# FFN gate and up computed as rows of 384 columns and turned back, and all q rows in one PSUM tile, in a decode-attention kernel

## Chip, cores, metric

One NeuronCore of a Trainium2 chip. The metric is device time in microseconds (us) of the one core. The kernel before takes 297.3 us (median of 3 runs, 297.22 to 297.4).

## The reference, cut

```python
# B = 2 sequences, one token each, D = 640, 32 heads of 192, window of 2048 keys, F = 1536
h  = x + attention(layernorm(x), k_cache, v_cache, wq, wo)   # scores and softmax over the last 2048 keys
h2 = h + (gelu(layernorm(h) @ w_gate) * (layernorm(h) @ w_up)) @ w_down
```

K and V of the window are 2 x 32 x 2048 x 192 bf16 values each, about 50 MB each. With the weights the core has to read 122.3 MB. The arithmetic for two tokens is small.

## The kernel before

All loads go through one ring of 120 KB per partition, from one DMA queue, in a fixed order: the first K tile, wq, then K and V tiles in turn with wo's four parts between, then w_gate, w_up and w_down. A load is issued as soon as the ring's place is free. For each K tile PE makes transposes, scores and the product with V; these hide behind the loads. At the very end comes the FFN: hnT, the second layernorm's output turned into columns, goes into gate and up; uT, the product of GELU(gate) and up, goes into w_down; h_rows adds h to the output's bank. Each matmul below is two records of PE, a weight load and a product. Two more words of the DMA packets: a packet of the kind "instruction" is a fetch of an engine's instructions, and a completion write is the 4-byte packet with which one of the 16 DMA engines ends its part of a load. Queue q1 carries the loads; q8 brings PE's instructions, one packet of 16384 bytes for about 265 PE records on average; q14 brings other instructions.

q, before: four PSUM tiles, four copies, 48 products that turn q into stationaries.

```python
for J in range(4):                      # q rows: 80 products in all
    for r in range(4):
        e.matmul(tps[J][32*r:32*(r+1), 0:384], lhsT=xnT[:, c, :], rhs=wq[...], tile_position=(0, 32*r))
# ... four ACT copies qrow[:, J] <- tps[J]; then for each J, hl, k (48 products):
e.matmul(ops_[:, col:col+15:2], lhsT=qx[:, o:o+255:2], rhs=selq[:, :])
```

FFN, before: the weights are the stationary, the result comes out in columns, so nothing has to be turned.

```python
def ffn_in(bank, key):                  # 60 products of 2 columns, for gate and again for up
    for f in range(NF):
        for c in range(NC5):
            e.matmul(bank[:, 2*f:2*f+2], lhsT=wv[:, c, 512*(f//4)+f%4 : 512*(f//4)+512 : 4], rhs=hnT[:, c, :])
# gate -> gsb -> GELU on DVE and ACT -> ga ; h_rows ; up -> uT = up * ga
for i, (f0, f1) in enumerate(WDC):      # ((0,4),(4,8),(8,10),(10,12)): 4 loads of w_down
    e.matmul(m1[32*r:32*r+2, 0:160], lhsT=uT[:, f, :], rhs=wd[...], tile_position=(0, 32*r))
# yrow <- m1, two stores of the output
```

A helper records the operations and adds the semaphore waits. Two engines that use the same PSUM bank are always put in order (the X list of an operation names the banks).

Of the kernel before, what the change touches and what calls it, by code (L numbers as in the profile page):

```python
# [12 lines left out]
B = 2  # L13
# [133 lines left out]
WDC = ((0, 4), (4, 8), (8, 10), (10, 12))  # L147
# [3 lines left out]
def bass_sequential_preLN__sliding_block_cached__geglu_ffn__decode_kernel(  # L151
# [12 lines left out]
    with ExitStack() as ctx:  # L164
# [23 lines left out]
        selq = sb("selq", [128, 8], BF16)  # L188
# [3 lines left out]
        bits = sb("bits", [128, 10], I32)  # L192
        pti = sb("pti", [128, 10], I32)
        pf = sb("pf", [128, 10], F32)
# [13 lines left out]
        xnT = sb("xnT", [128, NC5, 32], BF16)  # L208
        hnT = sb("hnT", [128, NC5, B], BF16)
        hT = sb("hT", [128, NC5, B], F32)  # L210
        qrow = sb("qrow", [128, 4, 2, 2, DH], BF16)
# [17 lines left out]
        hsel = sb("hsel", [128, 2, B], F32)  # L229
        gsb = sb("gsb", [128, NF * B], F32)  # L230
# [63 lines left out]
        def load_ffn():  # L294
            for key, w in (("wg", B_w_gate), ("wu", B_w_up)):
                load(key, 2 * NC5 * F, w.rearrange("(p c) f -> p c f", c=NC5),
                     lambda v: v.rearrange("p (c f) -> p c f", c=NC5))
            wd = B_w_down.rearrange("(i p s) n -> i p s n", p=128, s=4)
            for i, (f0, f1) in enumerate(WDC):
                load(("wd", i), 2 * (f1 - f0) * D, wd[f0 // 4, :, f0 % 4:f0 % 4 + f1 - f0, :],  # L300
                     lambda v: v.rearrange("p (s n) -> p s n", n=D))
# [38 lines left out]
        BITS = (1, 2, 3, 12, 16, 28, 31, 32, 64, 96)  # L340
# [18 lines left out]
        def layernorm(src, src_tok, dst, dst_tok):  # L359
# [14 lines left out]
            dve(tt(dst[:, :, 0:B], dT[:, 0, :, :], lt[:, 1, :].unsqueeze(1).to_broadcast([128, NC5, B]), ALU.mult),  # L374
                R=["dT0", "lt1"], W=[dst_tok])

        def _x_T(e):
# [7 lines left out]
        layernorm(xT, "xT", xnT, "xnT")  # L385


        dve(tt(pti[:, :], pi[:, :].to_broadcast([128, 10]), bits[:, :], ALU.bitwise_and),
            R=["pi"] + [("bits", k) for k in range(10)], W=["pti"])
# [20 lines left out]
        dve(ts(pg[:, 9:10], rb(31), 4.0, ALU.mult, pg[:, 8:9], ALU.add), R=["pf", "cq"], W=["cqb"])  # L410
# [4 lines left out]
        dve(ts(selq[:, :], cf[:, 0, 0:8], pg[:, 9:10], ALU.is_equal), R=["cf0", "cqb"], W=["selq"])  # L415
# [62 lines left out]
        def q_rows():  # L478
            for i, (c0, c1) in enumerate(WQC):
                wq, wtoks = where["wq", i]  # L480

                def fn(e, c0=c0, c1=c1, wq=wq):
                    for c in range(c0, c1):
                        for J in range(4):
                            for r in range(4):
                                ins = e.matmul(tps[J][32 * r:32 * (r + 1), 0:384], lhsT=xnT[:, c, :],  # L486
                                               rhs=wq[:, c - c0, 1536 * J + 384 * r:1536 * J + 384 * (r + 1)],
                                               start=(c == 0), stop=(c == NC5 - 1), tile_position=(0, 32 * r))
                    return ins

                pe(fn, R=["xnT"] + wtoks, X=[("t", J) for J in range(4)])
                done(("wq", i))
            for J in range(4):
                act(lambda e, J=J: e.activation(  # L494
                    out=qrow[:, J, :, :, :],
                    in_=tps[J][:, 0:384].rearrange("p (h d) -> p h d", h=2).unsqueeze(2).to_broadcast([128, 2, 2, DH]),
                    func=ACT.Copy, scale=SCALE), W=[("qrow", J)], X=[("t", J)])

        def q_stationary():
            for J in range(4):  # L500
                def fn(e, J=J):
                    for hl in range(2):
                        qx = qrow[:, J, hl, :, :].rearrange("p r d -> p (r d)")
                        for k in range(6):
                            col = 96 * J + 16 * k + hl
                            o = 256 * (k // 2) % DH + k % 2
                            ins = e.matmul(ops_[:, col:col + 15:2], lhsT=qx[:, o:o + 255:2], rhs=selq[:, :],  # L507
                                           start=True, stop=True)
                    return ins

                pe(fn, R=[("qrow", J), "selq"], X=["o"])
            for g in range(NG):
                x = 4 * (2 * (g % 2) + g % 4 // 2)
# [260 lines left out]
```

## Time and profile before

| what | value | view |
|---|---|---|
| time | 297.3 us | runs |
| span of the profiled execution | 295.3 us | page |
| main DMA queue | 97.1% of 16 engines' span, 122.29 MB | page, part 3 |
| chain of waits | DMA 74%, PE 19% | page, part 4 |
| hnT ready to uT started | 283.24 to 288.31, 5.07 us | timeline |
| last down products released | 292.17 us | timeline, chain |

From the page of the kernel before: the busy line; the clock granted to PE and the data rate in 40 slices of the span; the DMA queues (packets, MB, share of 16 engines); the shares of the chain of waits by engine; and one line of DMA issues (count, size, median time from issue to landing).

```profile
PE 199.6 (68%) x2251; PEld 158.1 (54%) x2251; DVE 126.9 (43%) x313; ACT 99.8 (34%) x126; POOL 2.7 (1%) x18
...
PEclk9998758997979589977888599979597979597565
...
GB/s 267 443 457 422 429 426 422 426 428 429 425 438 431 439 429 422 426 422 424 425 435 436 429 433 428 432 426 426 432 429 425 429 428 429 429 425 425 422 391 65
...
q1 hardware_dynamic: 6488, 122.29, 97.1%
q8 instruction: 17, 0.28, 0.4%
q14 instruction: 3, 0.02, 0.0%
...
DMA 74%; PE 19%; DVE 3%; ACT 2%; SPq 1%; issue 0%
...
ring<-in_A_k_cache_dram SPq DMA_DIRECT2D x16, 3072.0 KB, 27.2
```

The rate does not fall between the first slice and the last two. A K tile lands 27 us after its issue although 3 MB take about 7.3 us at this rate, so several transfers always stand in the queue; a computation that ends a few us earlier in the middle lets nothing arrive earlier. What remains is the end. From the timeline of the kernel before (start, duration, engine, line, operation, output and inputs, count, and in brackets what ended the idle time before it):

```profile
283.07 0.17 DVE L323 TENSOR_TENSOR hnT<-dT,lt 128x10 bf16<-128x10 f32 x1 [1.01 <-ACT lt L373]
283.30 2.16 PE L675 MATMUL sps<-hnT,ring 128*128 128x2 bf16 x60 [0.79 <-DVE hnT L323]
...
286.04 2.16 PE L675 MATMUL ops<-hnT,ring 128*128 128x2 bf16 x60
...
288.31 0.18 DVE L323 TENSOR_TENSOR uT<-ops,ga 128x24 bf16<-128x24 f32 x1 [0.96 <-PE ops L675]
...
288.55 0.70 PE L705 MATMUL m<-ring,uT 128*2 128x160 bf16 x16 [0.34 <-DVE uT L323]
...
290.59 1.23 PE L705 MATMUL m<-ring,uT 128*2 128x160 bf16 x24 [1.33 <-DMA ring<-in_B_w_down_dram]
...
292.17 0.44 PE L705 MATMUL m<-ring,uT 128*2 128x160 bf16 x8 [0.35 <-DMA ring<-in_B_w_down_dram]
292.66 0.32 DVE L711 CAST yrow<-m 98x160 bf16<-98x160 f32 x1 [4.17 <-PE m L705]
293.01 0.65 SPq L713 DMA_DIRECT2D out_dram<-yrow  x1
```

uT is there at 288.5, but PE then waits for w_down three times. The chain of waits (start, length, what) says the same:

```profile
263.40 28.73 DMA ring<-in_B_w_down_dram
292.13 0.04 issue
292.17 0.47 PE m L705 x8
```

The 48 down products without the waits would end near 290.3 instead of 292.6: the FFN has some 2.3 us of slack behind the last load. And why does that load land so late? The single DMA packets in the trace answer it. 15 of the 16 engines have finished by 290.2 us. One goes on alone, 2560 bytes every 0.10 us, to 291.69. Its two packets of 5120 bytes before that took 547 and 349 ns instead of 199, and they follow directly on an instruction fetch of 16384 bytes that ran from 288.16 to 289.23:

```
kernel before, packets (start us, ns, bytes):
288.16 1071 16384 (queue 8, instruction)   289.21 547 5120   289.75 349 5120
then 2560 bytes at 290.10 290.20 290.30 ... 291.59, one at a time; last completion write 291.69
```

### The profile page before, as it was taken

Reading aid. Unit: us, or ns where it says so; the run is one execution under the profiler, and the core shown is the slowest. Engines: PE = TensorE matmul, PEld = TensorE weight load, DVE = VectorE, ACT = ScalarE, POOL = GpSimd, SP = SyncE. Lnnn points to the kernel's source line nnn. Section 1 sums busy time; section 2 is a strip of 40 time slices with the busy share of each in tenths; the row PEclk is TensorE's granted clock in tenths of the full one; section 3 lists DMA queues with packets and bytes.
Section 4 is the critical chain, followed back from the end, with each engine's and each line's share of the span. In section 5 each row is a group of like instructions: output and inputs, shape, how many; then the busy total and the mean of one; then the engine's idle time right before and its main releaser. Section 6 shows DMA issues by size and latency. Waiting matters only on the chain.

```text
span 295.3 us, 5104 instructions
## 1 busy us (share of the span) xinstructions
PE 199.6 (68%) x2251; PEld 158.1 (54%) x2251; DVE 126.9 (43%) x313; ACT 99.8 (34%) x126; POOL 2.7 (1%) x18
## 2 busy tenths in 40 slices
PE   2583659849495397849591697567696876785773
PEld 1461348729293385538471676364676674753461
DVE  5940274725255154434344156335266434252230
ACT  2150316625253062516261244334244344241000
POOL 3000000000000000000000000000000000000000
PEclk9998758997979589977888599979597979597565
DMA  7999999999999999999999999999999999999991
GB/s 267 443 457 422 429 426 422 426 428 429 425 438 431 439 429 422 426 422 424 425 435 436 429 433 428 432 426 426 432 429 425 429 428 429 429 425 425 422 391 65
DMA packets 6520, 122.60 MB, mean 415 GB/s; under 512 B 738, under 2 KB 740, under 8 KB 1252
## 3 DMA queue, kind: packets, MB, share of 16 engines
q1 hardware_dynamic: 6488, 122.29, 97.1%
q8 instruction: 17, 0.28, 0.4%
q14 instruction: 3, 0.02, 0.0%
q10 hardware_dynamic: 12, 0.00, 0.0%
HBM read 122.29 MB, written 0.00 MB: 414 GB/s over the span
## 4 chain that ended last, share of the span: by engine, by line
DMA 74%; PE 19%; DVE 3%; ACT 2%; SPq 1%; issue 0%
DMA ring<-in_A_k_cache_dram 54%; PE tps L464 17%; DMA ring<-in_B_w_down_dram 10%; DMA ring<-in_A_wq_dram 9%; SPq L268 1%; ACT qrow L494 1%; PE ops L565 1%; DVE rq L323 1%; ACT ktr L473 1%; PE m L611 0%; PE m L594 0%; PE m L549 0%; PE tps L486 0%; DVE ktr L476 0%; DVE cf L323 0%
## 5 line engine op out<-in xcount | busy, mean ns | idle before, releaser
L464 PE MATMUL tps<-identf,ring 128*128 128x128 f32 x768 | 118.6, 325 | 48.1 <-DMA ring<-in_A_k_cache_dram 47.6
L464 PEld LDWEIGHTS tps<-identf,ring 128*128 128x128 f32 x768 | 109.4, 171 | 51.4 <-DMA ring<-in_A_k_cache_dram 48.9
L473 ACT ACTIVATE ktr<-tps 128x1024 bf16<-128x1024 bf16 x80 | 79.5, 1023 | 86.9 <-PE tps L464 86.9
L476 DVE COPY ktr<-tps 128x1024 bf16<-128x1024 bf16 x112 | 74.2, 688 | 76.4 <-PE tps L464 75.4
L540 ACT ACTIVATE eexp<-sm,nm 128x512 bf16<-128x512 f32 x16 | 11.5, 722 | 63.4 <-DVE nm L538 63.4
L529 DVE CUSTOM_DVE_ANT_1 sm<-sps,mska 128x512 f32<-128x512 f32 x16 | 11.1, 691 | 38.7 <-PE sps L523 38.7
L565 PE MATMUL ops<-ring,ering 128*32 128x384 bf16 x512 | 23.9, 328 | 3.6 <-DMA ring<-in_A_v_cache_dram 3.5
L523 PE MATMUL sps<-ktr,rq 128*16 128x512 bf16 x384 | 25.9, 404 | 0.4 <-DVE rq L323 0.4
L565 PEld LDWEIGHTS ops<-ring,ering 128*32 128x32 bf16 x512 | 12.5, 96 | 11.8 <-DMA ring<-in_A_v_cache_dram 4.6
L523 PEld LDWEIGHTS sps<-ktr,rq 128*16 128x16 bf16 x384 | 9.4, 90 | 11.3 <-issue 2.0
L536 PEld LDWEIGHTS m<-mrhs,pm 128*128 128x128 bf16 x16 | 1.5, 96 | 24.4 <-DVE mrhs L319 23.3
L536 PE MATMUL m<-mrhs,pm 128*128 128x16 bf16 x16 | 2.9, 184 | 16.9 <-DVE mrhs L319 16.1
L486 PE MATMUL tps<-ring,xnT 128*32 128x384 bf16 x80 | 5.1, 406 | 7.0 <-DMA ring<-in_A_wq_dram 5.8
L323 DVE TENSOR_TENSOR rq<-ops,mask 128x96 bf16<-128x96 f32 x16 | 2.7, 245 | 15.2 <-PE ops L507 15.2
L323 DVE TENSOR_TENSOR ering<-m,mask 128x256 bf16<-128x256 f32 x16 | 6.7, 420 | 3.2 <-PE m L549 3.2
L486 PEld LDWEIGHTS tps<-ring,xnT 128*32 128x32 bf16 x80 | 2.3, 113 | 9.6 <-DMA ring<-in_A_wq_dram 6.9
L323 DVE TENSOR_TENSOR orow<-m,wm 128x1536 bf16<-128x1536 f32 x4 | 7.0, 1757 | 0.1
L494 ACT ACTIVATE qrow<-tps 128x768 bf16<-128x768 f32 x4 | 2.9, 816 | 11.0 <-PE tps L486 11.0
L594 PE MATMUL m<-selb,orow 128*128 128x2 bf16 x48 | 3.5, 200 | 4.1 <-DVE orow L323 2.5
L371 ACT ACTIVATE lt<-m,eps_t 128x2 f32<-128x2 f32 x2 | 0.5, 262 | 16.5 <-PE m L369 16.5
L549 PE MATMUL m<-sel,eexp 128*128 128x64 bf16 x64 | 5.0, 206 | 1.2 <-ACT eexp L540 1.2
L594 PEld LDWEIGHTS m<-selb,orow 128*128 128x128 bf16 x48 | 3.2, 163 | 4.6 <-DVE orow L323 2.6
(100 smaller groups left out, 85.8 us busy)
## 6 DMA issues: line engine op xcount, KB each, us to landing
ring<-in_A_k_cache_dram SPq DMA_DIRECT2D x16, 3072.0 KB, 27.2
ring<-in_A_v_cache_dram SPq DMA_DIRECT2D x16, 3072.0 KB, 29.6
ring<-in_A_wo_dram SPq DMA_DIRECT2D x4, 1920.0 KB, 30.9
ring<-in_A_wq_dram SPq DMA_DIRECT2D x2, 3072.0 KB, 21.1
ring<-in_B_w_gate_dram SPq DMA_DIRECT2D x1, 1920.0 KB, 33.8
ring<-in_B_w_up_dram SPq DMA_DIRECT2D x1, 1920.0 KB, 24.6
ring<-in_A_wq_dram SPq DMA_DIRECT2D x1, 1536.0 KB, 27.9
ring<-in_B_w_down_dram SPq DMA_DIRECT2D x2, 640.0 KB, 26.9
```

The source lines that it names most:

```text
L323: return lambda e: e.tensor_tensor(out=out, in0=a, in1=b, op=op)
L464: ins = e.transpose(tps[bi][:, 128 * u:128 * (u + 1)], kv[:, off:off + 128], identf[:, :])
L473: act(lambda e, dst=dst, bv=bv: e.activation(out=dst, in_=bv, func=ACT.Copy), W=[("kt", slot, n)], X=[("t", bi)])
L476: dve(lambda e, dst=dst, bv=bv: e.tensor_copy(dst, bv), W=[("kt", slot, n)], X=[("t", bi)])
L486: ins = e.matmul(tps[J][32 * r:32 * (r + 1), 0:384], lhsT=xnT[:, c, :], rhs=wq[:, c - c0, 1536 * J + 384 * r:1536 * J + 384 * (r + 1)], st ...
L494: act(lambda e, J=J: e.activation(out=qrow[:, J, :, :, :], in_=tps[J][:, 0:384].rearrange("p (h d) -> p h d", h=2).unsqueeze(2).to_broadca ...
L523: ins = e.matmul(sps[32 * ch:32 * ch + 16, :], lhsT=rq[:, g, k, :], rhs=ktr[:, g % 2, k // 2, 1024 * ch + k % 2:1024 * (ch + 1):2], start= ...
L529: dve(lambda e: e.tensor_tensor_reduce(out=sm[:, :].rearrange("p (u x) -> p u x", u=4), in0=sps[:, :].rearrange("p (u x) -> p u x", u=4), ...
L540: act(lambda e: e.activation(out=eexp[:, :], in_=sm[:, :], func=ACT.Exp, bias=nm[:, 0:1], scale=1.0, accum_out=zr[:, g // 4 % 2, g % 4:g % ...
L549: ins = e.matmul(o, lhsT=eexp[:, 128 * u:128 * (u + 1)], rhs=sel64[:, :], start=True, stop=True)
L565: ins = e.matmul(ops_[32 * r:32 * (r + 1), 0:384], lhsT=ering[:, g % 4, t, :], rhs=vv[:, 384 * t:384 * (t + 1)], start=(g % 4 == 0 and t < 4),
L594: ins = e.matmul(m2[:, 2 * kk:2 * kk + 2], lhsT=orow[:, :, kk:DH:12], rhs=selb[:, :], start=True, stop=True)
```

## The change

Its intent is fewer and longer PE instructions. q: all rows of all heads in one PSUM tile, one copy instead of four, 12 products instead of 48. FFN: gate and up in 20 products of 384 columns each, in four column groups, instead of 60 products of two columns; the price is that the result stands in rows and has to be copied out of PSUM and turned back by three transposes. w_down is loaded in four equal parts. PE has 110 weight loads and 110 products fewer. Cut to its core:

```diff
-WDC = ((0, 4), (4, 8), (8, 10), (10, 12))
+WDC = ((0, 3), (3, 6), (6, 9), (9, 12))
-        BITS = (1, 2, 3, 12, 16, 28, 31, 32, 64, 96)
+        BITS = (1, 2, 3, 6, 12, 16, 28, 31, 32, 64, 96)
-        dve(ts(pg[:, 9:10], rb(31), 4.0, ALU.mult, pg[:, 8:9], ALU.add), R=["pf", "cq"], W=["cqb"])
+        dve(ts(pg[:, 9:10], rb(6), rb(1), ALU.add), R=["pf"], W=["cqa"])
+        dve(ts(pg[:, 9:10], pg[:, 9:10], 4.0, ALU.mult, pg[:, 8:9], ALU.add), R=["cqa", "cq"], W=["cqb"])
 # q rows: xnT now holds the two tokens four times at different columns, so that J picks the row
-    ins = e.matmul(tps[J][32 * r:32 * (r + 1), 0:384], lhsT=xnT[:, c, :], ...
+    ins = e.matmul(tps[0][32 * r:32 * (r + 1), 0:384], lhsT=xnT[:, c, 32 * J:32 * (J + 1)], ...
 # ... one ACT copy for all J, 12 products for the stationaries instead of 48 ...
+        def ffn_in(bank, xt, key):
+            wv, wtoks = where[key]
+            def fn(e):
+                for c in range(NC5):
+                    for r in range(4):
+                        ins = e.matmul(bank[32 * r:32 * r + 2, 0:384], lhsT=hnT[:, c, :], rhs=wv[:, c, 384 * r:384 * (r + 1)],
+                                       start=(c == 0), stop=(c == NC5 - 1), tile_position=(0, 32 * r))
+                return ins
+            pe(fn, R=["hnT"] + wtoks, X=[xt])
+        def ffn_columns(bank, xt, i):
+            act(lambda e: e.activation(out=grow[0:98, 192:384], in_=bank[0:98, 192:384], func=ACT.Copy), W=[("grow", 1)], X=[xt])
+            dve(lambda e: e.tensor_copy(grow[0:98, 0:192], bank[0:98, 0:192]), W=[("grow", 0)], X=[xt])
+            def fn(e):
+                for j in range(3):
+                    ins = e.transpose(tps[i][:, 128 * j:128 * j + 98], grow[0:98, j:384:3], identf[0:98, 0:98])
+                return ins
+            pe(fn, R=[("grow", 0), ("grow", 1), "identf"], X=[("t", i)])
 # order: gate, h_rows, gate's columns, GELU ; up, up's columns, uT ; down
```

More of the change, by code (lines that the diff above doesn't have):

```diff
@@ L187, in bass_sequential_preLN__sliding_block_cached__geglu_ffn__decode_kernel @@
         sel64 = sb("sel64", [128, 64], BF16)
-        selq = sb("selq", [128, 8], BF16)
+        selq = sb("selq", [128, 32], BF16)
         selb = sb("selb", [128, 2], BF16)
@@ L191, in bass_sequential_preLN__sliding_block_cached__geglu_ffn__decode_kernel @@
         pi = sb("pi", [128, 1], I32)
-        bits = sb("bits", [128, 10], I32)
-        pti = sb("pti", [128, 10], I32)
-        pf = sb("pf", [128, 10], F32)
+        bits = sb("bits", [128, 11], I32)
+        pti = sb("pti", [128, 11], I32)
+        pf = sb("pf", [128, 11], F32)
         pg = sb("pg", [128, 13], F32)
@@ L207, in bass_sequential_preLN__sliding_block_cached__geglu_ffn__decode_kernel @@
         lt = sb("lt", [128, 2, B], F32)
-        xnT = sb("xnT", [128, NC5, 32], BF16)
+        xnT = sb("xnT", [128, NC5, 136], BF16)
         hnT = sb("hnT", [128, NC5, B], BF16)
         hT = sb("hT", [128, NC5, B], F32)
-        qrow = sb("qrow", [128, 4, 2, 2, DH], BF16)
+        qrow = sb("qrow", [128, 2, 2, DH], BF16)
         rq = sb("rq", [128, NG, 6, 16], BF16)
@@ L229, in bass_sequential_preLN__sliding_block_cached__geglu_ffn__decode_kernel @@
         hsel = sb("hsel", [128, 2, B], F32)
+        grow = sb("grow", [128, 384], F32)
         gsb = sb("gsb", [128, NF * B], F32)
@@ L297, in load_ffn @@
                      lambda v: v.rearrange("p (c f) -> p c f", c=NC5))
-            wd = B_w_down.rearrange("(i p s) n -> i p s n", p=128, s=4)
+            wd = B_w_down.rearrange("(r p j) n -> r p j n", p=128, j=3)
             for i, (f0, f1) in enumerate(WDC):
-                load(("wd", i), 2 * (f1 - f0) * D, wd[f0 // 4, :, f0 % 4:f0 % 4 + f1 - f0, :],
+                load(("wd", i), 2 * (f1 - f0) * D, wd[i],
                      lambda v: v.rearrange("p (s n) -> p s n", n=D))
@@ L373, in layernorm @@
             act(lambda e: e.activation(out=lt[:, 1, :], in_=lt[:, 0, :], func=ACT.Exp, scale=-0.5), R=["lt0"], W=["lt1"])
-            dve(tt(dst[:, :, 0:B], dT[:, 0, :, :], lt[:, 1, :].unsqueeze(1).to_broadcast([128, NC5, B]), ALU.mult),
-                R=["dT0", "lt1"], W=[dst_tok])
+            n = dst.shape[2]
+            dve(tt(dst, dT[:, 0, :, :].unsqueeze(2).to_broadcast([128, NC5, n, B]),
+                   lt[:, 1, :].unsqueeze(1).unsqueeze(1).to_broadcast([128, NC5, n, B]), ALU.mult), R=["dT0", "lt1"], W=[dst_tok])
         def _x_T(e):
@@ L384, in bass_sequential_preLN__sliding_block_cached__geglu_ffn__decode_kernel @@
         dve(lambda e: e.tensor_copy(xT[:, :, :].rearrange("p c b -> p (c b)"), m2[:, 0:10]), W=["xT"], X=["m2"])
-        layernorm(xT, "xT", xnT, "xnT")
-        dve(tt(pti[:, :], pi[:, :].to_broadcast([128, 10]), bits[:, :], ALU.bitwise_and),
-            R=["pi"] + [("bits", k) for k in range(10)], W=["pti"])
+        layernorm(xT, "xT", xnT[:, :, :].rearrange("p c (j x) -> p c j x", j=4)[:, :, :, 0:B], "xnT")
+        dve(tt(pti[:, :], pi[:, :].to_broadcast([128, 11]), bits[:, :], ALU.bitwise_and),
+            R=["pi"] + [("bits", k) for k in range(11)], W=["pti"])
         dve(lambda e: e.tensor_copy(pf[:, :], pti[:, :]), R=["pti"], W=["pf"])
@@ L413, in bass_sequential_preLN__sliding_block_cached__geglu_ffn__decode_kernel @@
         dve(ts(pg[:, 12:13], rb(32), rb(31), ALU.add), R=["pf"], W=["c63"])
-        dve(ts(selq[:, :], cf[:, 0, 0:8], pg[:, 9:10], ALU.is_equal), R=["cf0", "cqb"], W=["selq"])
+        dve(ts(selq[:, :], cf[:, 0, 0:32], pg[:, 9:10], ALU.is_equal), R=["cf0", "cqb"], W=["selq"])
         dve(lambda e: e.tensor_copy(ef[:, :], ei[:, :]), R=["ei"], W=["ef"])
@@ L485, in fn @@
                             for r in range(4):
-                                ins = e.matmul(tps[J][32 * r:32 * (r + 1), 0:384], lhsT=xnT[:, c, :],
+                                ins = e.matmul(tps[0][32 * r:32 * (r + 1), 0:384], lhsT=xnT[:, c, 32 * J:32 * (J + 1)],
                                                rhs=wq[:, c - c0, 1536 * J + 384 * r:1536 * J + 384 * (r + 1)],
-                                               start=(c == 0), stop=(c == NC5 - 1), tile_position=(0, 32 * r))
+                                               start=(c == 0 and J == 0), stop=(c == NC5 - 1 and J == 3), tile_position=(0, 32 * r))
@@ L489, in fn @@
                     return ins
-                pe(fn, R=["xnT"] + wtoks, X=[("t", J) for J in range(4)])
+                pe(fn, R=["xnT"] + wtoks, X=[("t", 0)])
                 done(("wq", i))
-            for J in range(4):
-                act(lambda e, J=J: e.activation(
-                    out=qrow[:, J, :, :, :],
-                    in_=tps[J][:, 0:384].rearrange("p (h d) -> p h d", h=2).unsqueeze(2).to_broadcast([128, 2, 2, DH]),
-                    func=ACT.Copy, scale=SCALE), W=[("qrow", J)], X=[("t", J)])
@@ L499, in q_stationary @@
-        def q_stationary():
-            for J in range(4):
-                def fn(e, J=J):
-                    for hl in range(2):
-                        qx = qrow[:, J, hl, :, :].rearrange("p r d -> p (r d)")
-                        for k in range(6):
-                            col = 96 * J + 16 * k + hl
-                            o = 256 * (k // 2) % DH + k % 2
-                            ins = e.matmul(ops_[:, col:col + 15:2], lhsT=qx[:, o:o + 255:2], rhs=selq[:, :],
-                                           start=True, stop=True)
-                    return ins
-                pe(fn, R=[("qrow", J), "selq"], X=["o"])
+            act(lambda e: e.activation(
+                out=qrow[:, :, :, :],
+                in_=tps[0][:, 0:384].rearrange("p (h d) -> p h d", h=2).unsqueeze(2).to_broadcast([128, 2, 2, DH]),
+                func=ACT.Copy, scale=SCALE), W=["qrow"], X=[("t", 0)])
@@ new lines, in q_stationary @@
+        def q_stationary():
+            def fn(e):
+                for hl in range(2):
+                    qx = qrow[:, hl, :, :].rearrange("p r d -> p (r d)")
+                    for k in range(6):
+                        o = 256 * (k // 2) % DH + k % 2
+                        ins = e.matmul(ops_[:, 64 * k + hl:64 * k + 64:2], lhsT=qx[:, o:o + 255:2], rhs=selq[:, :],
+                                       start=True, stop=True)
+                return ins
+            pe(fn, R=["qrow", "selq"], X=["o"])
@@ L512, in q_stationary @@
             for g in range(NG):
-                x = 4 * (2 * (g % 2) + g % 4 // 2)
-                src = ops_[:, 96 * (g // 4):96 * (g // 4 + 1)].rearrange("p (k x) -> p k x", k=6)[:, :, x:x + 4]
+                x = 16 * (g // 4) + 8 * (g % 2) + 4 * (g % 4 // 2)
+                src = ops_[:, 0:384].rearrange("p (k x) -> p k x", k=6)[:, :, x:x + 4]
                 dve(tt(rq[:, g, :, :].rearrange("p k (q t) -> p k q t", q=4), src.unsqueeze(3).to_broadcast([128, 6, 4, 4]),
@@ L666, in bass_sequential_preLN__sliding_block_cached__geglu_ffn__decode_kernel @@
         h_columns()
-        layernorm(hT, "hT", hnT, "hnT")
-        def ffn_in(bank, key):
-            wv = where[key][0]
+        layernorm(hT, "hT", hnT[:, :, :].unsqueeze(2), "hnT")
+        def ffn_in(bank, xt, key):
+            wv, wtoks = where[key]
             def fn(e):
-                for f in range(NF):
-                    for c in range(NC5):
-                        ins = e.matmul(bank[:, 2 * f:2 * f + 2], lhsT=wv[:, c, 512 * (f // 4) + f % 4:512 * (f // 4) + 512:4], rhs=hnT[:, c, :],
-                                       start=(c == 0), stop=(c == NC5 - 1))
-                return ins
-            return fn
@@ L680, in bass_sequential_preLN__sliding_block_cached__geglu_ffn__decode_kernel @@
-        pe(ffn_in(sps, "wg"), R=["hnT"] + where["wg"][1], X=["s"])
-        dve(lambda e: e.tensor_copy(gsb[:, :], sps[:, 0:2 * NF]), W=["gsb"], X=["s"])
+                for c in range(NC5):
+                    for r in range(4):
+                        ins = e.matmul(bank[32 * r:32 * r + 2, 0:384], lhsT=hnT[:, c, :], rhs=wv[:, c, 384 * r:384 * (r + 1)],
+                                       start=(c == 0), stop=(c == NC5 - 1), tile_position=(0, 32 * r))
+                return ins
+            pe(fn, R=["hnT"] + wtoks, X=[xt])
@@ new lines, in ffn_columns @@
+        def ffn_columns(bank, xt, i):
[6 more added lines that the diff above has]
+            pe(fn, R=[("grow", 0), ("grow", 1), "identf"], X=[("t", i)])
+            return tps[i][:, 0:384].rearrange("p (j r y) -> p r j y", j=3, y=32)[:, :, :, 0:2]
@@ new lines, in h_rows, with rjb @@
+        def h_rows(e):
+            for r in range(4):
+                ins = e.matmul(m1[32 * r:32 * r + 2, 0:160], lhsT=hsel[0:98, r // 2, :], rhs=hrow[0:98, 160 * (r % 2):160 * (r % 2) + 160],
+                               start=True, stop=False, tile_position=(0, 32 * r), skip_group_check=True)
+            return ins
+        def rjb(t):
+            return t.rearrange("p (r j b) -> p r j b", r=4, j=3)
+        ffn_in(sps, "s", "wg")
+        pe(h_rows, R=["hrow", ("hsel", 0), ("hsel", 1)], X=["m1"])
@@ L682, in bass_sequential_preLN__sliding_block_cached__geglu_ffn__decode_kernel @@
+        gT = ffn_columns(sps, "s", 0)
+        dve(lambda e: e.tensor_copy(rjb(gsb[:, :]), gT), W=["gsb"], X=[("t", 0)])
         dve(tt(ga[:, 0, :], gsb[:, :], gsb[:, :], ALU.mult), R=["gsb"], W=["ga0"])
@@ L688, in bass_sequential_preLN__sliding_block_cached__geglu_ffn__decode_kernel @@
         dve(tt(ga[:, 0, :], ga[:, 1, :], gsb[:, :], ALU.mult), R=["ga1", "gsb"], W=["ga0"])
-        def h_rows(e):
-            for r in range(4):
-                ins = e.matmul(m1[32 * r:32 * r + 2, 0:160], lhsT=hsel[0:98, r // 2, :], rhs=hrow[0:98, 160 * (r % 2):160 * (r % 2) + 160],
-                               start=True, stop=False, tile_position=(0, 32 * r), skip_group_check=True)
-            return ins
-        pe(h_rows, R=["hrow", ("hsel", 0), ("hsel", 1)], X=["m1"])
-        pe(ffn_in(ops_, "wu"), R=["hnT"] + where["wu"][1], X=["o"])
-        dve(tt(uT[:, :, :].rearrange("p f b -> p (f b)"), ops_[:, 0:2 * NF], ga[:, 0, :], ALU.mult), R=["ga0"], W=["uT"],
-            X=["o"])
+        ffn_in(ops_, "o", "wu")
+        vT = ffn_columns(ops_, "o", 1)
+        dve(tt(uT[:, :, :].rearrange("p (r j) b -> p r j b", r=4), vT, rjb(ga[:, 0, :]), ALU.mult), R=["ga0"], W=["uT"], X=[("t", 1)])
         for i, (f0, f1) in enumerate(WDC):
```

## The prediction

> **What bounds the kernel.** DMA. The page's third part has the main queue's packets at 97.1% of 16 engines' span, 122.3 MB at about 427 GB/s in nearly every slice; the chain of waits is 74% DMA. No compute stage before the tail matters: in the list of who waits for whom, the DMA-issuing queue always waits for a ring slot with some 27 us of transfers (issue to landing) still queued in front. So the q half of the change saves time that nothing pays for.
>
> **q half, costed from the timeline.** Now: 4 ACT copies of 128x768 (2.92 us) with 48 q-stationary products between, 31.3 to 34.8 us. After: one copy (0.82) and 12 products (0.46): 2.2 us shorter. The 80 q products stay. I expect 0 us of this in the time; K1's transposes and one DMA issue come some 2 us earlier, behind a full queue.
>
> **FFN half.** At the end the granted clock is 0.50 (windows). Now gate takes 2.16 us for 60 products, up the same. After: 20 products of 384 columns; the o-projection's 48 of 320 columns took 3.53 us there, 65 ns each, so 384 columns about 80 ns: 20 take about 2.0 us with the last one's latency. That saves nearly nothing, and adds per bank: half copies on ACT and DVE (about 0.36; 160 columns took 0.32, 384 on ACT 0.49), three fp32 transposes (about 0.7 to 0.8; one is 0.42 here and they follow at about 0.2), semaphores, 0.2 for a strided copy. So gsb comes about 1.1 us later, uT at about 289.7 instead of 288.5 us. The down products (48, about 2.0 us) then end near 291.8, if w_down has landed. They end now at 292.64, because the last chunk, released at 292.17, is waited for. So the slower FFN chain just fits into the slack behind DMA. The last chunk grows from 8 to 12 rows' products: +0.15 us if it still ends last.
>
> **The tail of DMA, which decides.** In the trace's DMA packets, 15 engines end by 290.2 us; one alone runs 2560-byte packets (102 ns each) until 291.69. It is the engine whose 5120-byte packets took 547 and 349 ns (199 is usual) right after the 17th instruction fetch, 16384 bytes at 288.16 us, 1.07 us. The Trainium skill ("Runtime: NRT & Kernel Launch", Instruction fetch mechanics) has an engine's instructions refilled in 16 KiB blocks of 256 instructions; the trace agrees roughly: about 265 PE records between fetches. The change removes about 72 PE records in q and 148 in the FFN, so this last fetch should not happen, and the 16th slips from 278.1 to about 284. Then the last landing can be near 290.2 instead of 291.7, unless the 16th fetch hits one of the late engines; the end is then set by the FFN chain.
>
> **Sum.** -0.8 us if the FFN chain ends last, about -0.3 or +0.2 if DMA still does. I predict 296.7 us, range 295.9 to 297.6. Faster by over 2%: 0.01; within 2%: 0.98; slower: 0.01.
>
> **What shows it right or wrong.** Right: 16 instruction packets; GB/s per slice unchanged; q chain about 2 us shorter; uT 0.8 to 1.6 us later; down products waiting for w_down less or not at all; K and V waits unchanged. Wrong: 17 instruction packets, with w_down still ending the chain near 292.1; uT after 290.5, so the FFN chain lengthens the end; or a changed DMA rate.
>
> **What would make it wrong.** The transposes or strided PSUM reads costing far more at half clock; the 16th fetch falling on a late engine; 3840-byte packets slower than 5120 and 2560; a clock granted differently in the tail.

## The result and the profile after

The kernel after takes 297.36 us (median of 6 runs, 297.1 to 298.14) against 297.26 (297.05 to 297.4) for the kernel before; ratio 1.0009, 95% interval 0.9996 to 1.0022. Here and below a ratio is the mean time of one kernel's runs over that of the other's of the same rounds, so it is not quite the ratio of the medians. The change is worth nothing that can be told from zero. The profiled execution (298.14 us) is the slowest of the six, which has to be kept in mind when absolute times are read from it.

From the page after, the same parts:

```profile
PE 199.5 (67%) x2141; PEld 155.9 (53%) x2141; DVE 127.9 (43%) x316; ACT 98.4 (33%) x125; POOL 2.7 (1%) x19
...
PEclk9996559996979589989788699979795979795555
...
q1 hardware_dynamic: 6488, 122.29, 96.8%
q8 instruction: 17, 0.28, 0.4%
q14 instruction: 4, 0.03, 0.0%
...
DMA 69%; PE 24%; DVE 4%; ACT 1%; issue 1%; SPq 1%; DVEq 0%; ACTq 0%
```

The work moved from DMA to PE in the chain, without getting shorter. PE has 220 records fewer and is busy as long as before. The end of the timeline after:

```profile
284.57 0.17 DVE L324 TENSOR_TENSOR hnT<-dT,lt 128x10 bf16<-128x10 f32 x1 [1.27 <-ACT lt L374]
...
284.80 1.77 PE L675 MATMUL sps<-ring,hnT 128*2 128x384 bf16 x20 [0.85 <-DVE hnT L324]
...
286.62 0.33 ACT L682 ACTIVATE grow<-sps 98x192 f32<-98x192 f32 x1 [2.08 <-PE sps L675]
287.05 0.36 DVE L683 COPY grow<-sps 98x192 f32<-98x192 f32 x1 [2.31 <-ACT grow L682]
...
287.46 0.76 PE L687 MATMUL tps<-identf,grow 98*128 98x98 f32 x3 [0.36 <-DVE grow L683]
...
288.15 1.77 PE L675 MATMUL ops<-ring,hnT 128*2 128x384 bf16 x20
...
289.97 0.33 ACT L682 ACTIVATE grow<-ops 98x192 f32<-98x192 f32 x1 [0.63 <-PE ops L675]
290.40 0.36 DVE L683 COPY grow<-ops 98x192 f32<-98x192 f32 x1 [0.29 <-ACT grow L682]
...
290.82 0.76 PE L687 MATMUL tps<-identf,grow 98*128 98x98 f32 x3 [0.90 <-DVE grow L683]
...
291.69 0.18 DVE L324 TENSOR_TENSOR uT<-tps,ga 128x24 bf16<-128x24 f32 x1 [0.93 <-PE tps L687]
...
291.93 1.77 PE L722 MATMUL m<-ring,uT 128*2 128x160 bf16 x48 [0.34 <-DVE uT L324]
293.75 0.32 DVE L728 CAST yrow<-m 98x160 bf16<-98x160 f32 x1 [1.88 <-PE m L722]
```

Three things are to be seen.

1. The 48 down products run in one piece. PE no longer waits for w_down at all. The packets show why: the last bytes of w_down are in at 290.34, 1.35 us earlier than before, and no engine is left alone: the eight slowest finish between 289.9 and 290.34, the other eight by 289.1. The last instruction fetch comes at 293.2, behind them.
2. From hnT ready (284.74) to uT started (291.69) it is 6.95 us, 1.9 more than before (5.07). 20 products of 384 columns take 1.77 us, little less than the 2.16 us of the 60 short ones; then come the copies and transposes.
3. The DVE half of each copy starts only when the ACT half has ended ("<-ACT grow"). The two halves were meant to run together. They read the same bank, and the program orders accesses by bank. The Trainium skill ("PSUM — Partial Sum Buffer", PSUM bank collisions raise a hardware error) says that two engines may not use the same bank and 32-partition quadrant at once, reads against reads included. The trace agrees with the consequence: 0.33 + 0.10 + 0.36 us in a row. A version that drops the order was not run, nor one that splits the copy by quadrants of partitions instead of columns; what they would bring stays open.

hnT itself comes 1.5 us later than in the profile before. The last V product took 2.75 us here and 1.62 before, under a granted clock of 0.50 from 266.9 us on. In the profiles of the experiments below hnT is ready between 283.4 and 284.6, with either form of the FFN, so I take this for scatter from execution to execution; the FFN change itself lies behind hnT. The kernel before has the earliest hnT of the 14 profiles (283.24; the others 283.4 to 284.7).

### The profile page after: what moved, and what is told of

Its sections match the earlier page's. It is cut to its first block, busy times and chain, and to the rows that moved or that the text cites. A ratio compares the mean times of both kernels' runs of the same rounds, so it can differ in the third digit from the quotient of the medians. Undisturbed runs are those within 1.5% of the kernel's fastest.

```text
span 296.4 us, 4893 instructions
## 1 busy us (share of the span) xinstructions
PE 199.5 (67%) x2141; PEld 155.9 (53%) x2141; DVE 127.9 (43%) x316; ACT 98.4 (33%) x125; POOL 2.7 (1%) x19
## 4 chain that ended last, share of the span: by engine, by line
DMA 69%; PE 24%; DVE 4%; ACT 1%; issue 1%; SPq 1%; DVEq 0%; ACTq 0%
DMA ring<-in_A_k_cache_dram 37%; DMA ring<-in_A_v_cache_dram 22%; PE tps L467 14%; DMA ring<-in_A_wq_dram 9%; PE ops L565 3%; PE m L611 1%; DVE rq L324 1%; PE m L594 1%; SPq L269 1%; PE m L722 1%; PE sps L675 1%; DVE orow L324 1%; PE ops L675 1%; PE m L579 1%; PE tps L687 1%
## 5 line engine op out<-in xcount | busy, mean ns | idle before, releaser
L467 PE MATMUL tps<-identf,ring 128*128 128x128 f32 x768 | 117.4, 323 | 47.4 <-DMA ring<-in_A_k_cache_dram 46.8
L467 PEld LDWEIGHTS tps<-identf,ring 128*128 128x128 f32 x768 | 108.2, 169 | 50.5 <-DMA ring<-in_A_k_cache_dram 48.1
L565 PE MATMUL ops<-ring,ering 128*32 128x384 bf16 x512 | 25.0, 339 | 6.1 <-DMA ring<-in_A_v_cache_dram 6.0
L489 PE MATMUL tps<-ring,xnT 128*32 128x384 bf16 x80 | 5.7, 444 | 7.6 <-DMA ring<-in_A_wq_dram 7.6
L549 PEld LDWEIGHTS m<-sel,eexp 128*128 128x128 bf16 x64 | 4.8, 112 | 1.7 <-DVE nm L538 1.3
```

Source lines behind the costliest of these rows:

```text
L467: ins = e.transpose(tps[bi][:, 128 * u:128 * (u + 1)], kv[:, off:off + 128], identf[:, :])
L489: ins = e.matmul(tps[0][32 * r:32 * (r + 1), 0:384], lhsT=xnT[:, c, 32 * J:32 * (J + 1)], rhs=wq[:, c - c0, 1536 * J + 384 * r:1536 * J + ...
L549: ins = e.matmul(o, lhsT=eexp[:, 128 * u:128 * (u + 1)], rhs=sel64[:, :], start=True, stop=True)
L565: ins = e.matmul(ops_[32 * r:32 * (r + 1), 0:384], lhsT=ering[:, g % 4, t, :], rhs=vv[:, 384 * t:384 * (t + 1)], start=(g % 4 == 0 and t < 4),
```

## The experiments

My theory after the result had two parts. **Fetch**: before the change, instruction fetches make one DMA engine late, and the change takes this away. **Chain**: what is won is used up by the longer chain from hnT to uT. Rivals: that the q half costs something; that the late engine has nothing to do with fetches. Twelve kernels were run, all correct.

In this table of all of them, "fetches" is the number of 16384-byte fetches that started before 289.9 us, "next" the start of the first one after that, "last" the last completion write of the w_down loads, all from the packets of the profiled execution; "store" is the time from the output's store instruction until its wait on SP ends, "8 KB fetch" the start of the last 8192-byte fetch (q14).

| kernel | median us | fetches | next | last | 8 KB fetch | store |
|---|---|---|---|---|---|---|
| before | 297.25 | 17 | - | 291.70 | 296.4 | 1.86 |
| after | 297.36 | 16 | 293.2 | 290.35 | 291.5 | 1.69 |
| q_only | 298.26 | 16 | 290.2 | 291.35 | 294.4 | 2.70 |
| q_only_pad36 | 298.09 | 17 | - | 291.63 | 294.1 | 2.80 |
| pad92 | 297.24 | 17 | 290.2 | 291.73 | 296.5 | 1.68 |
| ffn_only | 297.78 | 16 | 291.1 | 290.35 | 291.8 | 1.68 |
| q_only_b7 | 296.76 | 16 | 290.1 | 291.48 | 296.5 | 1.68 |
| pad78 | 297.25 | 17 | 290.3 | 291.81 | 296.5 | 1.67 |
| after_one | 296.85 | 16 | 292.2 | 290.36 | 294.3 | 2.51 |
| after_best | 297.33 | 16 | 291.5 | 290.34 | 293.7 | 2.67 |
| after_best_b7 | 296.76 | 16 | 292.0 | 290.31 | 295.5 | 1.86 |
| q_b7_late | 297.26 | 16 | 290.2 | 291.82 | 296.6 | 1.69 |
| mixed | 296.18 | 16 | 290.1 | 290.31 | 295.6 | 1.68 |
| mixed_pad130 | 297.43 | 17 | 291.3 | 291.85 | 296.6 | 1.67 |

### First round: each half alone, and idle products

**q_only**: the q half of the diff, with the old FFN and the old w_down parts.

> The q half alone, with the old FFN and the old w_down chunks. Fetch theory (the end of the kernel before is held up by the 17th instruction fetch, which lands on one DMA engine at 288.2 us and delays it to 291.7 us): with 72 fewer PE records this fetch comes only when the weights have landed, w_down's last landing moves from 291.7 to about 290.3 us, the last down products start near 291 instead of 292.17 us, and the time is 0.8 to 1.5 us below before, about 296.2 us. Rival (the q half is off the critical path and the tail is what it was): 297.3 us, no difference beyond 0.2 us.

Measured: 298.26 us (6 runs, five of them 298.14 to 298.43, one 297.05), ratio 1.0025 (1.0011 to 1.0038). Both theories missed: this half costs 1 us. The data were all in at 290.38, but a fetch stood at 290.24 to 291.34 in front of one engine's completion write, which came at 291.35. That explains why nothing was won, not why 1 us was lost. The loss is in the store. Of q_only, the line of the page for the second instruction queue, and below it, from the list of who waited for whom on SP (total, times, longest), the wait for the store:

```profile
q14 instruction: 4, 0.03, 0.0%
```

```profile
SPq L732 <- DMA out_dram<-yrow: 2.0, 1, 2.0
```

In the packets the 8192-byte fetch runs from 294.41 to 294.96. Three of the store's four packets on each of the two queues pass at 294.5 to 294.7; the fourth starts at 294.95 and 294.97, just when the fetch ends.

**q_only_pad36**: q_only plus 36 products without use.

```diff
             def fn(e):                       # e_columns(g)
+                for _ in range(3 if g in range(1, 13) else 0):
+                    e.matmul(m2[:, 300:302], lhsT=identb[:, :], rhs=identb[:, 0:2], start=True, stop=True)
```

> The q half alone, plus 36 idle products (72 PE records) spread over tiles 1 to 12 where PE waits for K anyway, so that PE has as many records as the kernel before. Fetch theory: a fetch falls at about 288 us again and the gain of q_only is gone: within 0.2 us of before, 297.3 us. Rival (whatever q_only gains comes from the shorter q chain itself): the same time as q_only.

Measured: 298.09 us (297.97 to 298.31), ratio 1.0027. It has the late engine of the kernel before (17 fetches, last at 288.1, end of loads at 291.63, packets of 548 and 346 ns) and the late store of q_only. The time says little, since the store's microsecond lies over it; the packets say that with the number of PE records of before, the late engine of before comes back.

**pad92**: the kernel before with 7 such products on each of 13 tiles.

> The kernel before with 91 idle products (182 PE records, nearly a block of 256 less 72) spread over tiles 1 to 13, nothing else. Fetch theory: only the place of the fetches against the tail counts, so this one, with more work, gains like q_only: one fetch near 284 us, the next after the last landing, 0.5 to 1.5 us below before, about 296.3 us. Rival (more PE work is never faster here): 297.3 us or a little more.

Measured: 297.24 us, ratio 0.9999. The expected gain did not come. The fetches stood where I had wanted them, at 280.9 and 290.2, and still one engine ran alone until 291.72, with no lengthened packet in the tail. So the place of the last fetch is not what matters: the fetch theory as I had written it fell.

**ffn_only**: the FFN half with the old q part.

> The FFN half alone with the old q part (148 fewer PE records). Chain theory (after the change the end is set by the longer gate and up chain, not by DMA): hnT to uT takes about 6.9 us as after the change (5.0 before), uT near 290.5 to 291.7 us, the down products run without a wait for w_down, and the time is that of the whole change, 297.1 to 297.8 us. Rival (the q half costs something that hides the gain of the FFN half): at least 0.5 us below before.

Measured: 297.78 us (297.61 to 298.37), ratio 1.0021 (1.0009 to 1.0033). As the chain theory expects: loads in at 290.35, no wait for w_down; hnT ready at 283.85 and uT started at 291.15, 7.3 us.

### Second round: the store, and the chain

**q_only_b7**: one DVE instruction fewer, same values (6 and 1 are disjoint bits, so their sum is the mask 7).

```diff
-        dve(ts(pg[:, 9:10], rb(6), rb(1), ALU.add), R=["pf"], W=["cqa"])
-        dve(ts(pg[:, 9:10], pg[:, 9:10], 4.0, ALU.mult, pg[:, 8:9], ALU.add), R=["cqa", "cq"], W=["cqb"])
+        dve(ts(pg[:, 9:10], rb(7), 4.0, ALU.mult, pg[:, 8:9], ALU.add), R=["pf", "cq"], W=["cqb"])
```

> The q half alone with one DVE instruction fewer: the row index modulo 8 comes from one mask of 7 instead of the sum of two masks, same values. Store theory (in q_only the one additional DVE instruction brings an 8192-byte instruction fetch forward from 296.4 to 294.4 us, onto the output's store, whose landing then takes 2.7 us instead of 1.9): the fetch goes back behind the end, the store lands in 1.9 us again, and the time falls from 298.2 to 297.1 to 297.5 us. Rival (the q half is slower for another reason, such as its w_down landing): stays near 298.2 us.

Measured: 296.76 us, ratio 0.9982 (0.9965 to 0.9999). The same two lines, for q_only_b7:

```profile
q14 instruction: 3, 0.02, 0.0%
```

```profile
SPq L731 <- DMA out_dram<-yrow: 1.0, 1, 1.0
```

The fetch went from 294.4 to 296.5, behind the end, and the wait on the store fell by 1.0 us, as did the time of most runs. One small DVE instruction at about 10 us had cost 1 us at 294 us. Over all kernels of the table the pattern holds without exception: fetch at 293.7 to 294.4, store 2.5 to 2.8 us; fetch elsewhere, 1.7 to 1.9. Why the store is late by 0.8 us or more when its last packet is late by 0.3 is not shown.

The six runs are in two groups, 295.82 to 296.26 and 297.27 to 297.43. The profiled one is of the slower group, with a fetch from 290.12 to 291.20 in front of one engine's last packet of 2560 bytes. That the faster three escaped it is likely but was not seen.

**pad78**: as pad92, with 6 products per tile.

> The kernel before with 78 idle products (156 PE records) instead of the 91 of pad92. Fetch theory, mended: in pad92 the last fetch came at 290.2 us, still in front of one engine's last bytes, and so nothing was won; 26 records later it comes at 290.7 us or after, when 15 or 16 engines have finished, the last w_down bytes are there at about 290.4 us and the time is 0.6 to 1.4 us below before, near 296.2 us. Rival (the late engine is late for its own reasons, not for a fetch): 297.2 us as pad92.

Measured: 297.25 us (297.21 to 297.33). Again one engine runs alone to 291.80, before and while the fetch of 290.3 runs; it is not the engine that carries that fetch. My mended place theory fell too. What pad92, pad78, q_only_pad36 and the kernel before have in common is seen in the table: 17 fetches before the last weights, where the kernels without the lone late engine have 16. There are 16 DMA engines. This is the **count** theory: the fetches go round the engines, and the engine that has carried one more than the others is late by the end, wherever that fetch fell. (The fourth round mends one part of it: only eight of the engines carry them.)

**after_one**: the whole change, each bank copied whole by ACT.

```diff
-            act(lambda e: e.activation(out=grow[0:98, 192:384], in_=bank[0:98, 192:384], func=ACT.Copy), W=[("grow", 1)], X=[xt])
-            dve(lambda e: e.tensor_copy(grow[0:98, 0:192], bank[0:98, 0:192]), W=[("grow", 0)], X=[xt])
+            act(lambda e: e.activation(out=grow[0:98, :], in_=bank[0:98, 0:384], func=ACT.Copy), W=[("grow", 0), ("grow", 1)], X=[xt])
```

> The whole change, but each bank is copied whole by ACT (98x384) instead of half by ACT and then half by DVE. Chain theory (the FFN chain ends last and the two half copies run one after the other because they read one bank): 0.49 us instead of 0.33 + 0.10 + 0.36 per bank, so hnT to uT falls from 6.9 to about 6.3 us and the time by about 0.5 us to 296.8 us. Rival (the end is set by w_down's landing also after the change): no difference, 297.3 us.

Measured: 296.85 us, but scattered from 296.4 to 298.56, ratio 0.9998 (0.9977 to 1.0019): by its time this is inconclusive. Its profile, from the timeline:

```profile
286.22 0.49 ACT L682 ACTIVATE grow<-sps 98x384 f32<-98x384 f32 x1 [2.08 <-PE sps L675]
286.76 0.77 PE L686 MATMUL tps<-identf,grow 98*128 98x98 f32 x3
```

0.54 us from the copy's start to the transposes instead of 0.84, for each of the two banks; hnT ready to uT is 6.35 us instead of 6.95, as expected. But with fewer DVE instructions after it, the 8192-byte fetch moved from 291.5, where it hurt nothing, to 294.3, onto the store. The repair of one thing set off another.

**after_best**: after_one with 8 of up's 20 products put ahead of gate's transposes.

```diff
         ffn_in(sps, "s", "wg")
         pe(h_rows, ...)
+        ffn_in(ops_, "o", "wu", 0, 2)      # row blocks 0 and 1
         gT = ffn_columns(sps, "s", 0)
         # ... GELU ...
-        ffn_in(ops_, "o", "wu")
+        ffn_in(ops_, "o", "wu", 2, NC5)
```

> As after_one, and up's first two of five row blocks (8 of 20 products) go ahead of gate's transposes, so that PE works while ACT copies the bank. Chain theory: another 0.3 to 0.6 us off hnT to uT, about 5.8 us, and about 296.5 us. Rival as for after_one: 297.3 us.

Measured: 297.33 us (296.52 to 297.71), ratio 0.9999. A miss: hnT to uT is 6.35 us, the same as after_one. The gap that these products were to fill, while ACT copies the bank, was already filled by h_rows. The store was late here too (2.67 us).

### Third round: a version built on both findings

**mixed**: the q half with the mask of 7; gate in columns as before the change, where nothing has to be turned and GELU can start at once; up in rows, one ACT copy, three transposes; w_down in four equal parts. Against after_one:

```diff
-        ffn_in(sps, "s", "wg")
+        def gate_columns(e):
+            wv = where["wg"][0]
+            for r in range(4):
+                for j in range(3):
+                    f = 3 * r + j
+                    for c in range(NC5):
+                        ins = e.matmul(sps[:, 2 * f:2 * f + 2], lhsT=wv[:, c, 384 * r + j:384 * (r + 1):3], rhs=hnT[:, c, :],
+                                       start=(c == 0), stop=(c == NC5 - 1))
+            return ins
+        pe(gate_columns, R=["hnT"] + where["wg"][1], X=["s"])
-        gT = ffn_columns(sps, "s", 0)
-        dve(lambda e: e.tensor_copy(rjb(gsb[:, :]), gT), W=["gsb"], X=[("t", 0)])
+        dve(lambda e: e.tensor_copy(gsb[:, :], sps[:, 0:2 * NF]), W=["gsb"], X=["s"])
         # and the mask of 7, as in q_only_b7
```

> A new version: the q half with the mask of 7, gate in columns as before the change (60 products, no transposes), only up in rows and turned back, its bank copied whole by ACT, w_down in thirds. Count theory (a DMA engine is late when it has carried one more 16 KiB instruction fetch than the others before the last weights are in; 16 fetches are harmless, the 17th makes one engine 1.4 us late): about 4380 PE records, only 16 fetches before 290.4 us, last landing 290.4, uT near 289.5, last down product near 291.3 to 291.6, store landing in 1.9 us since DVE has no more instructions than before; 296.0 to 296.4 us. Rivals: the FFN chain or the granted clock holds it at 297 us or above; or w_down still lands at 291.7 us.

Measured: 296.18 us (296.01 to 296.43) against 297.25, ratio 0.9963 (0.995 to 0.9976). It is the fastest of all by its median and steadier than the other variants of the change. From its timeline:

```profile
284.12 0.17 DVE L324 TENSOR_TENSOR hnT<-dT,lt 128x10 bf16<-128x10 f32 x1 [1.06 <-ACT lt L374]
284.35 1.82 PE L706 MATMUL sps<-hnT,ring 128*128 128x2 bf16 x60 [0.85 <-DVE hnT L324]
...
286.58 1.82 PE L674 MATMUL ops<-ring,hnT 128*2 128x384 bf16 x20
...
288.45 0.49 ACT L681 ACTIVATE grow<-ops 98x384 f32<-98x384 f32 x1 [1.16 <-PE ops L674]
...
289.86 0.18 DVE L324 TENSOR_TENSOR uT<-tps,ga 128x24 bf16<-128x24 f32 x1 [1.80 <-PE tps L685]
290.10 1.77 PE L729 MATMUL m<-ring,uT 128*2 128x160 bf16 x48 [0.34 <-DVE uT L324]
291.92 0.33 DVE L735 CAST yrow<-m 98x160 bf16<-98x160 f32 x1 [1.88 <-PE m L729]
```

hnT to uT is 5.57 us; the down products run through without a wait, since the loads are in at 290.3; the store takes 1.68 us. A 17th fetch ran from 290.14 to 291.23, but on an engine with nothing left to do.

**after_best_b7**: after_best with the mask of 7.

> after_best with the mask of 7, one DVE instruction fewer. Store theory: the 8192-byte fetch, which in after_best came at 293.7 us and made the store land in 2.7 us, goes behind the end of the kernel; the store lands in about 1.7 us and the median falls from 297.3 to about 296.5 us, with no run above 297.2. Rival (the scatter of after_best is the granted clock alone): unchanged, 297.3 us with runs at 297.7.

Measured: 296.76 us (296.35 to 297.62), ratio 0.999 (0.9978 to 1.0002). The fetch went to 295.5 and the store back to 1.86 us, as expected; that no run would be above 297.2 was wrong (297.24 and 297.62). The kernels whose PE chain ends last scatter more than the kernel before; the slowest runs of after, ffn_only, after_one and after_best_b7 have the lowest mean granted clock of their groups (0.817 to 0.822). That fits a chain on PE, but it was not tested.

**q_b7_late**: q_only_b7 with h_rows behind up's products.

> q_only_b7 with the four products that put the residual rows into the output bank moved behind up's products: the same instructions in another order. In q_only_b7 the 17th fetch came at 290.1 to 290.2 us and caught the last packet or the completion write of one engine; three of six runs took 295.8 to 296.3 us, three 297.3 to 297.4. If the fetch now comes 0.2 to 0.4 us later, more runs are of the fast kind: median near 296.1 us. If the order does not move the fetch, the same two groups as q_only_b7.

Measured: 297.26 us, again two groups (295.99 and 296.09; 297.26 to 297.44). The order did not move the fetch (290.2), so it tells nothing new.

### Fourth round: the count alone

**mixed_pad130**: mixed with 10 idle products on each of 13 tiles, 260 PE records, which is one block of 256 and four more. This leaves the tail and the fetches against it nearly where they were; only the number of fetches before it grows by one.

> mixed with 130 idle products (260 PE records, one fetch block of 256 and four) spread over tiles 1 to 13, where PE waits for K; the tail is the same, and the fetches fall at the same times against it, but one more lies in front of it. Count theory: 17 fetches before the last weights are in, as in the kernel before; one DMA engine runs alone to about 291.7 us, PE waits for w_down again, and the time is 297.0 to 297.4 us, as before. Place theory (what counts is whether a fetch falls into the last microseconds of the loads): fetches near 280.5 and 290.1 us as in mixed, last landing 290.3, 296.2 us as mixed.

Measured: 297.43 us (297.39 to 297.6), ratio 1.0007 (0.9993 to 1.0021): 1.25 us more than mixed (in another round; the kernel before took 297.25 in the one and 297.26 in the other). From its page and its timeline:

```profile
q8 instruction: 18, 0.29, 0.4%
```

```profile
287.62 1.77 PE L676 MATMUL ops<-ring,hnT 128*2 128x384 bf16 x20 [1.32 <-DMA ring<-in_B_w_up_dram]
...
290.86 0.18 DVE L324 TENSOR_TENSOR uT<-tps,ga 128x24 bf16<-128x24 f32 x1 [3.32 <-PE tps L687]
```

One engine ran alone to 291.85, at its usual pace; the last fetch before that began at 281.0, and the next at 291.3 did not slow it. And the lateness did not wait for w_down: up's products waited 1.3 us for w_up, so uT came 1.0 us later than in mixed, and the down products then ran without the wait for w_down that was expected. The idle products cannot have done this by their own time, because they stand in tiles 1 to 13, where the chain is made of K's loads. The count theory gave the number; the place theory (296.2 us) is out.

Five of five kernels with 17 fetches (the kernel before among them) have the lone late engine. Of the nine with 16, none has it except where the next fetch, at 290.1 to 290.2, stood directly in front of one engine's end (q_only, q_only_b7, q_b7_late).

The packet records do not name the engine, but the completion writes show how far each of the 16 engines is behind, and they correct the theory. Two loads of the kernel before:

```
us behind the load's first completion write, in order of time
after 9 fetches (first at 168.93):  0.00 0.03 0.04 0.10 0.14 0.24  0.65  1.58 1.58 1.60 1.61 1.63 1.67 1.73  2.00  3.19
after 15 fetches (first at 273.06): 0.00 0.00 0.04 0.05 0.13 0.19  0.64  1.63  1.98  3.10 3.11 3.14 3.15 3.17 3.17 3.26
```

After nine fetches seven engines are about 1.6 us behind and one about 3.2; after fifteen, seven are about 3.2 behind and one about 1.6; six stay level (the other two do not move with these fetches; they moved when the 8192-byte fetches came). All 14 profiles show this pattern. So each 16384-byte fetch puts the engine that carries it about 1.6 us behind for the rest of the run, and only eight of the 16 engines carry them, in turn. The packets give the same price: in mixed_pad130 the fetch at 280.99 took 1.10 us, and the load packet that follows on its end 1.03 us instead of 0.57, together 1.56 us. Sixteen fetches are therefore two full rounds of eight. They are not free: the eight engines that carried them end the loads at about 290.2, six others are done by 287.5. The 17th begins a third round and leaves one engine alone. An estimate from these numbers: with eight fetches instead of 16 the loads would end near 289.0, where the slower of the two other engines ends, 1.2 us earlier still. This was not run.

## Why the prediction was right or wrong

The measured 297.36 us lies in the stated range, and "within 2%" was right. The 0.6 us of gain in the middle of it did not come. Step by step:

- **DMA bounds the kernel, and the q half saves nothing that anybody pays for.** Right: the rate per slice is unchanged, and q's stationaries started 1.1 us earlier without any effect in the end. The shortening was 1.1 us instead of 2.2, since PE ran at half clock there in this execution (the last 16 q products took 1.47 us, not 0.83, and the 12 products 0.82, not 0.46).
- **The q half costs nothing either.** Not said, but assumed, and wrong: its one additional DVE instruction cost 1 us when it stood alone (q_only 298.26; without it 297.27 to 297.43 in the slower group of q_only_b7, which has the same fetch at 290.1 in its profile). In the whole change this was hidden by luck, since the FFN half's further DVE instructions moved the same fetch on to 291.5.
- **"the last landing can be near 290.2 instead of 291.7".** Right: 290.34.
- **"this last fetch should not happen", 16 instruction packets.** It happened at 293.2, behind the loads, and the 16th came at 281.0, not 284. And my reason was incomplete: a fetch in the tail does hold one engine, but so does one anywhere before, by about 1.6 us; what decided here is whether a 17th, the first of a third round over eight engines, comes before the last weights. The page's count of 17 in both profiles does not show the difference; the times of the packets do.
- **The FFN chain.** This is the step that failed: the term was mis-sized. I put the half copies at 0.36 us per bank, side by side; they ran one after the other and took 0.84 us from the first start to the transposes. With the rest of the sum, hnT to uT came to about 6.5 us, and it measured 6.95 (7.3 in ffn_only). The products (1.77 us against about 2.0) and the transposes (0.76 against 0.7 to 0.8) were sized well. after_one shows the size of the copies' part: 6.35 us. uT at 291.69 lies beyond the 290.5 that the prediction itself had named as the sign that the FFN chain lengthens the end. The chain did end last, but the 0.8 us forecast for this case did not come.
- **"the slower FFN chain just fits into the slack behind DMA".** It fitted into the slack of before, 2.3 us, by 0.4 us, but only for an hnT as early as in the profile before (283.24). DMA moved its own end forward by 1.35 us, so that the chain, 1.9 us longer, became the end. From then on whatever delays hnT from one execution to the next counts in full, where the slack had swallowed it before. This is worked out from single profiles; how early hnT is in the runs that were only timed was not seen. The prediction had started its sum from the hnT of one profile, which turned out to be the earliest of 14 by 0.1 us and earlier than their median by about 0.7. So the range held because it was wide: the DMA gain was foreseen, and the chain ate it.
- **"The last chunk grows": +0.15 us.** Played no part, since PE did not wait for the last part any more.

So the gain of the change was real on the side of DMA, and was turned into a new wait on PE; mixed, which keeps the first with a shorter chain (5.57 us) and the store undisturbed, takes the 1 us. What gate's form and the mask each gave in it was not separated.

## What to carry to other kernels

When a kernel is bound by DMA to the last microsecond, look at the single packets at the end and at the completion writes all along: the slowest of the 16 DMA engines ends the load, and here each 16 KB instruction fetch put one of eight of them about 1.6 us behind for good. So the number of instructions can matter even where the computing engine has time to spare, and even in a part of the program that ends long before. Shorter instruction counts are worth nothing if the result then has to be copied and turned on the path that ends last; keep the form without a turn where a long elementwise chain follows (gate), and use the other where none does (up). And when a harmless small edit costs a microsecond, see whether a fetch has moved onto the store.

## What the Trainium skill lacked or had wrong

- "Runtime: NRT & Kernel Launch", Instruction fetch mechanics, calls the cost of crossing a 16 KiB block "mostly hidden". For the sequencer that may be so; here each fetch holds one DMA engine for about 1.07 us (16384 bytes, where data of that size pass in about 0.61 us at the 26.9 bytes per ns of the K packets, worked out from the trace) and leaves it about 1.6 us behind, and the 17th of them cost 1.25 us of the kernel's time (mixed against mixed_pad130). The page does not say that fetches share the engines of the loads with this effect, and no page says that only eight of the 16 engines carry PE's fetches, as the completion writes of all 14 profiles show.
- The same section gives blocks of 16 KiB for all engines. The trace agrees for PE's (16384-byte packets, about 265 PE records apart), but the refills on the other instruction queue came as single packets of 8192 bytes (three or four in the span). One DVE instruction fewer moved the last of them by 2.1 us (q_only, q_only_b7), so these are DVE's, or follow DVE.
- No page tells of a fetch falling on the output's store: 2.5 to 2.8 us until it had landed instead of 1.7 to 1.9, in four kernels out of four.
- "DMA: Bandwidth & Descriptors", Queues, rings and completion order, has an engine alternate between its queues packet by packet. The runs agree and give the price: in q_only a 4-byte completion write stood behind a 16384-byte fetch from 290.24 to 291.34, and in q_only_b7 a packet of 2560 bytes from 290.12 to 291.20.
- "PSUM — Partial Sum Buffer" has the rule on one bank for two engines, for disjoint columns too, but not the price of keeping to it when a copy is split between ACT and DVE by columns: 0.33 and 0.36 us became 0.84 us with the waits, and one ACT copy of the whole, 0.49 us, was faster.
